# x kept by heads and turned with the unit matrix, quarters of w1 and w2 in halves, nine raw buffers for the first pieces

## The chip, the cores and the metric

One core of one Trainium2 chip. The metric is device time in microseconds (us) of one execution of the whole kernel, as the median of several runs. The engines are named as the profile names them: PE (TensorE: matmuls), PEld (its weight loads), DVE (VectorE), ACT (ScalarE), POOL (GpSimd), SP (SyncE, which here issues most DMAs).

## The reference

```python
def reference(x, state, w1, w2, w3, w_out, w_gate, w_val, w_out2):
    # x: 8 batches, 8 heads, 512 positions, 64; state: 8, 8, 32, 64
    a = softmax(scale * x @ state.T)          # 512 x 32 of each batch and head
    xread = a @ state
    a2 = softmax(scale * state @ x.T)         # 32 x 512
    sread = a2 @ x
    t = concatenate([xread, sread], axis=2)   # 8 x (512 + 32) rows = 4352 rows of 512
    h = ((t @ w1) * (t @ w2)) @ w3            # 512 -> 1024 -> 1024
    y = h @ w_out                             # 1024 -> 512
    return (sigmoid(y @ w_gate) * (y @ w_val)) @ w_out2     # 512 -> 1536 -> 512
```

x and state come in as float32, the weights of the two feed-forward blocks as float64, which the kernel turns into float32 by itself.

## The kernel before

The kernel has two large parts. The first goes through the eight batches in turn: the attention of a batch and the first feed-forward block of its 512 rows. The second does the second feed-forward block. PE works in order; what it is given, and in which order, is written out by hand.

**The batches.** While a batch's feed-forward block runs (`ffn1`, eight steps `j` with matmuls into `pab`, then four steps with matmuls into `py`), the attention of the next batch is put between its steps: `attention` returns small functions, and the dictionary `before` puts them into numbered slots. Slots 6 and 7 hold `xt`, two calls in each: one call turns two heads of x, so that the 64 columns of a head lie on partitions. Before the change one call is four transposes on PE of 128x128 (`turn`, line 289), for which x lies as `xn[p, pair, chunk, head of the pair, 64]`; ACT then copies the result to `xT`. Slot 8 holds `scores` (line 312, matmuls into `psc` on 64x32 parts of the array) and the softmax, and slots of the batch after it `a2t` (line 404), `sread` (line 421, `psr`, 128x32 parts) and `sreadt`. The products of state and weights (line 526, `psw`, 64x32 parts) are made there too: each `make(0, 1)` or `make(2, 3)` turns two quarters of w1 and w2 into the weights of the next batch, and `fetch` has the quarters loaded again from DRAM (`w12_d`).

x of a later batch is loaded by `load_x`, one DMA for each of the eight heads.

**The first batch.** `plan_start` has no other work to hide behind. It lists its steps with an engine, a cost in microseconds and what each depends on, and `Plan.order` turns the list into one order for all engines: among the steps that can begin first it takes the one with the longest path behind it. The engines then run what they got in order. In it

- `load_half` loads x in two DMAs as `xz`, and `place_x` lets ACT copy it into `xn` in four copies, one for each pair of heads; the turn of a pair waits for its copy (`placed`);
- `convert` loads one piece of 128x512 float64 numbers into a raw buffer and turns it into float32 (ACT: lines 196 and 197, DVE: lines 198, 202, 206). There are 40 such pieces: 16 of w1 and w2, 8 of w_out, 16 of w3. The raw buffers are a ring of seven (`raws`, `raw_tile`): three in the pool `cv`, two in `pw`, and two that later hold `aT`;
- `quarter(q)` converts four pieces into one tile `wq` (two such tiles), and has POOL store the tile to `w12_d` (line 656) as soon as it is full;
- `make(q)` multiplies a quarter with the state and `pab(j)` multiplies the result with the attention weights; in the first batch both are plain float32;
- `wo_split` splits a piece of w_out into a high part (ACT, tile `wo0`) and a low part (DVE, line 808, tiles `wol` on the places with the tag `sw1`), `w3_turn` turns and splits w3, and `wp_sum` multiplies the two (`pwp`); `u_split` splits the products of the first batch.

Of the kernel before, what the change touches and what calls it, by code (L numbers as in the profile page):

```python
# [8 lines left out]
F32 = mybir.dt.float32  # L9
# [108 lines left out]
def tile_state_attention__then__gated_ffns(  # L118
# [145 lines left out]
    with tc.manual_schedule(engines={mybir.EngineType.PE}):  # L264
# [3 lines left out]
        xn = {}  # L268

        def load_x(b):  # L270
            t = at.tile([P, G, SC, 2, D], F32, name="xn", bufs=2)
            xn[b] = t
            for h in range(H):
                nc.sync.dma_start(
                    out=t[:, h // 2, :, h % 2], in_=x[b, h].rearrange("(p c) d -> p c d", c=SC)
                )

        def attention(b, plain=False):

# [3 lines left out]
            def xt(g):  # L283
                def turn():
                    if g == 0:
                        t["xT"] = at.tile([P, G, S], F32, tag="xT", name="xT")
                    pt = t["pxt", g] = ps_at.tile([P, 512], F32, tag="at", name="pxt")
                    for c in range(SC):
                        nc.tensor.transpose(
                            pt[:, c * P : (c + 1) * P],  # L290
                            xn[b][:, g, c].rearrange("p a d -> p (a d)"),
                            ident,
                        )

                return [
                    ("pe", 0.44, turn),
                    ("act", 0.49, lambda: copy("act", t["xT"][:, g], t["pxt", g])),
                ]
# [116 lines left out]
            def sread():  # L415
                def products_():
                    pt = t["psr"] = ps_at.tile([P, 2, D], F32, tag="at", name="psr")
                    for k in range(2):
                        for c in range(SC):
                            for g in range(G):  # L420
                                nc.tensor.matmul(
                                    pt[NS * g : NS * g + NS, k],
                                    t["a2"][:, k, c, NS * g : NS * g + NS],
                                    xn[b][:, g, c, k],
                                    start=c == 0,
                                    stop=c == SC - 1,
                                )
# [67 lines left out]
            )  # L495

        def new_wq():
            return pb.tile([P, 2, G, WQ], F32, name="wq", bufs=2)

        def fetch(q):  # L500
            t = new_wq()
            nc.sync.dma_start(
                out=t.rearrange("p a g f -> p (a g f)"), in_=w12_d[q].rearrange("p a g f -> p (a g f)")
            )
            return t

        def behind(fn):
            with tc.issue_after(last["raw"].ins):
# [2 lines left out]
        class StateWeights:  # L511
# [9 lines left out]
            def product(self, q, pts):  # L521
                w = self.raw.pop(q)
                for a in range(2):
                    for g in range(G):
                        for k in range(2):
                            nc.tensor.matmul(
                                pts[k][NS * g : NS * g + NS, a * WQ : (a + 1) * WQ],
                                stT[64 * k : 64 * k + 64, g, self.b * NS : (self.b + 1) * NS],
                                w[64 * k : 64 * k + 64, a, g],
                                start=True,  # L530
                                stop=True,
                            )
# [27 lines left out]
        def plan_start(cur, nxt):  # L560
# [1 line left out]
            plan = Plan()  # L562
            add = plan.add
            b = cur.b
            raws, rs, ms, wqs = Ring(7), Ring(2), Ring(3), Ring(2)
            ats, mains, ys_, asbs, w3s = Ring(2), Ring(4), Ring(2), Ring(2), Ring(3)
            cell = {}

            def chain(parts, *deps):
                for engine, cost, fn in parts:  # L570
                    deps = (add(engine, cost, fn, *deps),)
                return deps[0]

            def raw_tile(n):
                if n % 7 < 3:
                    return cv.tile([P, 512, 2], U32, name="raw", bufs=3)
                if n % 7 < 5:
                    return pw.tile([P, 512, 2], U32, name="raw", bufs=2)
                return at.tile([P, 512, 2], U32, tag=f"aT{n % 7 - 5}", name="raw")

            def convert(src, place, *deps):
                n = len(raws.users)
                raw_free, raw_users = raws.take()
                r_free, r_users = rs.take()
                c = {}

                def load():
                    c["raw"] = raw_tile(n)
                    load_raw(c["raw"], src)

                def first():
# [20 lines left out]
                for j in range(4)  # L612
            ]

            def load_half(i):
                if i == 0:
                    cell["xz"] = at.tile([P, H, SC, D], F32, tag="xn", name="xz", bufs=2)
                h = i * H // 2
                nc.sync.dma_start(
                    out=cell["xz"][:, h : h + H // 2].rearrange("p h c d -> p h (c d)"),  # L620
                    in_=x[b, h : h + H // 2].rearrange("h (p c) d -> p h (c d)", c=SC),
                )

            xs = [add("sp", 0.48, lambda i=i: load_half(i), load=1.7) for i in range(2)]

            def place_x(g):
                if g == 0:
                    xn[b] = at.tile([P, G, SC, 2, D], F32, name="xn", bufs=2)
                copy("act", xn[b][:, g], cell["xz"][:, 2 * g : 2 * g + 2].rearrange("p a c d -> p c a d"))

            placed = []
            for g in range(G):
                placed.append(add("act", 0.52, lambda g=g: place_x(g), xs[g // 2], *placed[-1:]))

            wq_users = []

            def quarter(q):
                free, users = wqs.take()
                wq_users.append(users)
                out = []  # L640

                def place(i):
                    if i == 0:
                        cur.raw[q] = cell["wq", q] = new_wq()
                    a, h = divmod(i, 2)
                    return cell["wq", q][:, a, 2 * h : 2 * h + 2].rearrange("p g f -> p (g f)")

                for i in range(4):
                    a, h = divmod(i, 2)
                    src = (w1, w2)[a][2 * h * P : 2 * (h + 1) * P, 2 * q * WQ : 2 * (q + 1) * WQ]  # L650
                    d, _ = convert(src.rearrange("(k p) f -> p k f", p=P), lambda i=i: place(i), free, *out[:1])
                    out.append(d)

                def store():
                    t = cell["wq", q]
                    nc.gpsimd.dma_start(
                        out=w12_d[q].rearrange("p a g f -> p (a g f)"),
                        in_=t.rearrange("p a g f -> p (a g f)"),
                    )

                users.append(add("pool", 1.0, store, out, load=2 * LOAD))
                return out

            turned = []
            for g in range(G):
                free, users = ats.take()
                parts = xt(g)
                p = chain(parts[:1], free, placed[g])
                turned.append(chain(parts[1:], p))
                users.append(turned[-1])  # L670
            free, users = mains.take()
# [119 lines left out]
            for k in range(HALF):  # L791
                wo_load(k)
            w3_load(0)
            pab(6)
            pab(7)

            wo = {}

            def wo_tile(k, i):
                if "wo" not in cell:  # L800
                    cell["wo"] = pw.tile([P, JF, DM], F32R, name="wo0", bufs=1)
                    cell["wol"] = [
                        pb.tile([P, 2, DM], F32R, tag="sw1", name="wol", bufs=4) for _ in range(JF // 2)
                    ]
                return cell["wol"][k // 2][:, k % 2] if i else cell["wo"][:, k]

            def minus(o, x0, x1):
                nc.vector.tensor_tensor(out=o, in0=x0, in1=x1.bitcast(F32), op=ALU.subtract)

            def wo_split(k):  # L810
                a = add("act", 0.52, lambda: copy("act", wo_tile(k, 0), cell["wof", k]), wof[k])
                wo[k] = a, add(
                    "dve", 0.6, lambda: minus(wo_tile(k, 1), cell["wof", k], wo_tile(k, 0)), a
                )
# [90 lines left out]
            def u_split(j):  # L905
# [8 lines left out]
                a = add("act", 0.52, high, uw[j], [wo[k] for k in range(JF)], *cell.get("us", []))  # L914
                cell["us"] = [add("dve", 0.6, lambda: minus(t[1], cell["uw", j], t[0]), a)]

            for j in range(JF):
                u_split(j)

            add("sp", 6.7, lambda: load_x(order[1]), placed, load=3.0)  # L920
            for q in range(2):
                add("sp", 0.5, lambda q=q: nxt.fetch(q), wq_users[q + 2], load=3.0)

            engines = mybir.EngineType
            with tc.manual_schedule(
# [62 lines left out]
        class DirectWeights:  # L988
# [5 lines left out]
            def prep(self, j):  # L994
                q, jj = divmod(j, 2)
                if q not in self.raw:
                    self.raw[q] = fetch(q)
                f = self.raw[q][:, :, :, jj * P : (jj + 1) * P]
                t = [pb.tile([P, 2, KM, P], F32R, tag=f"sw{i}", name=f"dw{i}", bufs=4) for i in range(2)]
                for a in range(2):  # L1000
                    split(t[0][:, a], t[1][:, a], f[:, a])
                self.done[j] = t

            def weights(self, j):
# [633 lines left out]
```

## Time and profile before

| | us |
|---|---|
| median of 3 runs (1331.62 to 1333.92) | 1332.9 |
| the profiled execution | 1333.85 |
| its span, first to last instruction | 1332.1 |
| PE busy in it | 1299.9 (98%) |
| DVE busy | 847.7 (64%) |
| ACT busy | 678.9 (51%) |
| mean granted TensorE clock | 0.993 |

The profiled execution lies 0.95 us above the median. A busy PE is one that always has a matmul in flight. The share of the granted clock is of 2.4 GHz; 0.50 is 1.2 GHz.

### The profile page before, as it was taken

To read this page: it belongs to the slowest core of one execution; us is meant where nothing else is said; L and a number is where in the kernel's file an instruction comes from. 1 tells how busy PE (TensorE), PEld (TensorE's weight loads), DVE (VectorE), ACT (ScalarE), POOL (GpSimd) and SP (SyncE) were. 2 spreads that over 40 slices of the span, in tenths; PEclk is the share of its full clock that TensorE was granted. 3 is DMA by queue.
4 is the path that set the end of the run, shared out by engine and by line. 5 is a ranking of instruction groups with operands and counts; after the bars stand their busy time and mean duration, and the time that the engine had idled before them with its cause. 6 is when DMAs were issued, how large, how long until landed. Compare 5 with 4: busy or idle time off the path is not lost. (4 is left out here: it accounts for less than half of the span.)

```text
span 1332.1 us, 20278 instructions
## 1 busy us (share of the span) xinstructions
PE 1299.9 (98%) x7664; PEld 1090.8 (82%) x7664; DVE 847.7 (64%) x1519; ACT 678.9 (51%) x1347; POOL 133.9 (10%) x155
## 2 busy tenths in 40 slices
PE   4999999999999999999999999999999999999997
PEld 2487777778777779988899998888998988889995
DVE  5893554574574685186767776858777756657643
ACT  5993444455454574364555664643654542524521
POOL 0000000020202030012222101222211000000000
PEclk7999999999999999999999999999999999999999
DMA  8994342345463542824434567546355744133122
GB/s 292 347 279 132 114 156 73 142 150 196 170 206 143 214 171 85 316 90 149 139 127 162 176 258 266 174 141 219 135 194 190 277 181 162 48 127 126 52 95 71
DMA packets 122185, 224.67 MB, mean 169 GB/s; under 512 B 39912, under 2 KB 68072, under 8 KB 115432
## 3 DMA queue, kind: packets, MB, share of 16 engines
q1 hardware_dynamic: 87464, 163.08, 35.6%
q10 hardware_dynamic: 32896, 46.67, 10.2%
q0 software_dynamic: 1728, 13.63, 2.6%
q8 instruction: 60, 0.98, 0.3%
q14 instruction: 37, 0.30, 0.1%
HBM read 155.19 MB, written 68.16 MB: 168 GB/s over the span
## 5 line engine op out<-in xcount | busy, mean ns | idle before, releaser
L1425 PE MATMUL psA<-y,wt 128*128 128x384 f32 (+1 forms) x1440 | 301.0, 357 | 0.7 <-ACT sg L1450 0.5
L1522 PE MATMUL po<-wo,p 128*128 128x512 f32 x1224 | 281.3, 390 | 0.8 <-DVE p L1086 0.8
L1425 PEld LDWEIGHTS psA<-y,wt 128*128 128x128 f32 x1440 | 259.1, 188 | 25.3 <-ACT sg L1450 0.8
L1522 PEld LDWEIGHTS po<-wo,p 128*128 128x128 f32 x1224 | 229.2, 188 | 49.5 <-DVE p L1086 2.5
L1425 PE MATMUL psB<-y,wt 128*128 128x384 f32 (+1 forms) x720 | 159.5, 356 | 0.0
L158 ACT ACTIVATE u<-psA 128x384 f32<-128x384 f32 (+1 forms) x120 | 63.9, 532 | 159.1 <-PE psA L1425 140.3
L1425 PEld LDWEIGHTS psB<-y,wt 128*128 128x128 f32 x720 | 130.0, 188 | 11.2
L225 PE MATMUL py<-u,wp 128*128 128x512 f32 (+1 forms) x576 | 132.3, 381 | 0.8 <-DVE u L163 0.6
L225 PE MATMUL pab<-aT,sw 128*128 128x512 f32 x448 | 126.6, 404 | 0.8 <-DVE aT L163 0.8
L225 PEld LDWEIGHTS py<-u,wp 128*128 128x128 f32 x576 | 102.9, 188 | 26.2 <-issue 2.9
L964 DVE TENSOR_TENSOR asb<-asb,pab 128x512 f32<-128x512 f32 (+1 forms) x64 | 41.8, 653 | 115.7 <-PE pab L228 106.3
L158 ACT ACTIVATE p<-sg 128x384 fp32r<-128x384 f32 (+1 forms) x120 | 67.9, 567 | 80.6 <-DVE sg L1461 68.8
L163 POOL TENSOR_TENSOR o<-m,o 128x256 fp32r<-128x256 f32 x72 | 60.7, 843 | 436.1 <-ACT o L158 358.1
L225 PEld LDWEIGHTS pab<-aT,sw 128*128 128x128 f32 x448 | 81.1, 188 | 19.5 <-DVE aT L163 1.1
L1537 DVE TENSOR_TENSOR ob<-po,ob 128x512 f32<-128x512 f32 x68 | 46.7, 688 | 62.3 <-PE po L1522 59.3
L1452 DVE TENSOR_TENSOR sg<-psB,u 128x384 f32<-128x384 f32 (+1 forms) x60 | 36.4, 607 | 75.8 <-ACT u L158 75.7
L1425 PE MATMUL psC<-y,wt 128*128 128x384 f32 (+1 forms) x360 | 80.0, 357 | 0.3 <-DVE s L1458 0.2
L1086 DVE TENSOR_TENSOR p<-sg,p 128x384 fp32r<-128x384 f32 (+1 forms) x120 | 74.1, 617 | 3.9 <-ACT p L158 0.8
L1086 DVE TENSOR_TENSOR y<-yf,y 128x384 fp32r<-128x384 f32 (+1 forms) x112 | 68.3, 634 | 12.7 <-ACT y L158 11.5
L228 PE MATMUL pab<-aT,sw 128*128 128x512 f32 x224 | 70.6, 396 | 0.0
L1425 PEld LDWEIGHTS psC<-y,wt 128*128 128x128 f32 x360 | 64.8, 188 | 6.6 <-DVE s L1458 1.1
L158 ACT ACTIVATE y<-yf 128x384 fp32r<-128x384 f32 (+1 forms) x120 | 62.1, 556 | 11.3 <-DMA yf<-yd 10.5
(128 smaller groups left out, 1795.8 us busy)
## 6 DMA issues: line engine op xcount, KB each, us to landing
wq<-w12d SPq DMA_DIRECT2D x32, 1024.0 KB, 6.8
wt<-wd SPq DMA_DIRECT2D x12, 1792.0 KB, 9.0
part<-ob SPq DMA_DIRECT2D x68, 256.0 KB, 2.6
ob<-part SPq DMA_DIRECT2D x68, 256.0 KB, 3.7
raw<-in_moe_w SPq DMA_DIRECT2D x32, 512.0 KB, 5.6
wd<-o ACTq DMA_DIRECT2D x56, 256.0 KB, 2.1
yf<-yd SPq DMA_DIRECT2D x27, 384.0 KB, 3.9
yf<-yd SPq DMA_DIRECT2D x19, 512.0 KB, 4.7
```

The lines of the kernel that those rows point to most:

```text
L158: return nc.scalar.activation(out=o, in_=i, func=AF.Copy)
L163: (sub or nc.vector).tensor_tensor(out=lo, in0=src, in1=hi.bitcast(F32), op=ALU.subtract)
L225: nc.tensor.matmul(o, w[i], xx[k], start=begin and n == 0 and i + k == 0, stop=False)
L228: nc.tensor.matmul(o, w[1 - late], xx[late], start=False, stop=end and n == len(pairs) - 1)
L964: p2["dve"] = nc.vector.tensor_tensor(out=asb[:, :n], in0=asb[:, :n], in1=pab[1][:, :n], op=ALU.mult)
L1086: nc.vector.tensor_tensor(out=o, in0=x0, in1=x1, op=ALU.subtract)
L1425: nc.tensor.matmul(o, w[:, i, kb * P : (kb + 1) * P], xx[kb][h], start=start, stop=i == 1 and kb == 1, skip_group_check=True,)
L1452: nc.vector.tensor_tensor(out=t, in0=o, in1=kept[a, what], op=ALU.add)
L1522: nc.tensor.matmul(o, pt[j][i][:, s * P : (s + 1) * P], wot[j][:, h], start=j == js[0] and i + h == 0, stop=j == js[-1] and i == 1,)
L1537: nc.vector.tensor_tensor(out=ob, in0=o, in1=ob, op=ALU.add)
```

## The change

x now stays in one layout from load to use, `xn[p, head, chunk, 64]`, in every batch. It is loaded in two DMAs of four heads each, and the copies of `place_x` are gone. The turn of two heads is eight matmuls instead of four transposes: the 128x64 numbers of one head and one chunk are the weights, the 128x128 unit matrix is what moves, and the two heads of a pair go to the lower and the upper 64 partitions of the result. `sread` reads the new layout.

A quarter of w1 and w2 is now two tiles (w1's part and w2's part) of half the size, on four places. In `plan_start` quarters 0 and 1 lie there, quarters 2 and 3 on the four places tagged `sw1`. `fetch` and the stores to `w12_d` are two DMAs for each quarter where they were one. The stores of quarters 2 and 3 stand after the first piece of w3 in the list of steps; those of quarters 0 and 1 stand at its end and wait for the fourth piece of w_out.

The raw buffers: the first 16 pieces (w1 and w2) use nine, three in `cv`, two in `pw` and four on places tagged `wo0`; the 24 others use five, `cv` and `pw`. The high part of w_out, one tile before, is four tiles on the `wo0` places. `wo_split` of an even `k` therefore waits for the last user of the raw buffer there, and for the product and the stores of quarter 2 (`k` below 4) or quarter 3.

```diff
         def load_x(b):
-            t = at.tile([P, G, SC, 2, D], F32, name="xn", bufs=2)
-            xn[b] = t
-            for h in range(H):
-                nc.sync.dma_start(
-                    out=t[:, h // 2, :, h % 2], in_=x[b, h].rearrange("(p c) d -> p c d", c=SC)
-                )
+            for i in range(2):
+                load_half(b, i)
+
+        def load_half(b, i):
+            if i == 0:
+                xn[b] = at.tile([P, H, SC, D], F32, name="xn", bufs=2)
+            h = i * H // 2
+            nc.sync.dma_start(
+                out=xn[b][:, h : h + H // 2].rearrange("p h c d -> p h (c d)"),
+                in_=x[b, h : h + H // 2].rearrange("h (p c) d -> p h (c d)", c=SC),
+            )
...
                     for c in range(SC):
-                        nc.tensor.transpose(
-                            pt[:, c * P : (c + 1) * P],
-                            xn[b][:, g, c].rearrange("p a d -> p (a d)"),
-                            ident,
-                        )
+                        for k in range(2):
+                            nc.tensor.matmul(
+                                pt[D * k : D * k + D, c * P : (c + 1) * P],
+                                xn[b][:, 2 * g + k, c],
+                                ident,
+                                start=True,
+                                stop=True,
+                            )
...
         def new_wq():
-            return pb.tile([P, 2, G, WQ], F32, name="wq", bufs=2)
+            return pb.tile([P, G, WQ], F32, name="wq", bufs=4)
...
-            raws, rs, ms, wqs = Ring(7), Ring(2), Ring(3), Ring(2)
+            rs, ms = Ring(2), Ring(3)
...
+            def raw_slot(n):
+                if n < 4 * NQ:
+                    n %= 9
+                    return ("cv", n) if n < 3 else ("pw", n - 3) if n < 5 else ("wo", n - 5)
+                n = (n - 4 * NQ) % 5
+                return ("cv", n) if n < 3 else ("pw", n - 3)
...
-            placed = []
-            for g in range(G):
-                placed.append(add("act", 0.52, lambda g=g: place_x(g), xs[g // 2], *placed[-1:]))
...
-                users.append(add("pool", 1.0, store, out, load=2 * LOAD))
                 return out
+
+            def store(q, *deps):
+                for a in range(2):
+                    def go(a=a):
+                        nc.gpsimd.dma_start(
+                            out=w12_d[q][:, a].rearrange("p g f -> p (g f)"),
+                            in_=cell["wq", q][a].rearrange("p g f -> p (g f)"),
+                        )
+                    wq_users[q].append(add("pool", 1.0, go, quarters[q], *deps, load=LOAD))
...
-                p = chain(parts[:1], free, placed[g])
+                p = chain(parts[:1], free, xs[g // 2])
...
             w3_load(0)
+            store(2)
+            store(3)
             pab(6)
...
             def wo_split(k):
-                a = add("act", 0.52, lambda: copy("act", wo_tile(k, 0), cell["wof", k]), wof[k])
+                if k % 2 == 0:
+                    cell["free", k // 2] = [raw_slots.get(("wo", k // 2)), wq_users[2 + k // 4]]
+                a = add(
+                    "act", 0.52, lambda: copy("act", wo_tile(k, 0), cell["wof", k]), wof[k],
+                    cell["free", k // 2], wo[k - 1] if k % 2 else None,
+                )
...
+            store(0, wof[HALF - 1])
+            store(1, wof[HALF - 1])
             for j in range(JF):
                 u_split(j)
 
-            add("sp", 6.7, lambda: load_x(order[1]), placed, load=3.0)
+            add("sp", 1.7, lambda: load_x(order[1]), turned, load=3.0)
             for q in range(2):
-                add("sp", 0.5, lambda q=q: nxt.fetch(q), wq_users[q + 2], load=3.0)
+                add("sp", 0.5, lambda q=q: nxt.fetch(q), wq_users[q], load=3.0)
```

## Rows read from the trace of the kernel before

**Rows 1.** The page, part 1: busy us, share of the span, instructions.

```profile
PE 1299.9 (98%) x7664; PEld 1090.8 (82%) x7664; DVE 847.7 (64%) x1519; ACT 678.9 (51%) x1347; POOL 133.9 (10%) x155
```

**Rows 2.** Busy us (instructions) of each engine by stretch, granted clock, DMA share, GB/s.

```profile
70.00:80.00 10.00, 10.00 (x51) 8.24 (x50) 10.00 (x22) 9.51 (x17) 0.00 (x0) 1.00 0.87 294
...
400.00:450.00 50.00, 50.00 (x413) 39.28 (x412) 27.05 (x44) 27.72 (x50) 9.69 (x10) 1.00 0.47 169
```

**Rows 3.** PE in order of time, first and last turn slot: start us, us, instructions.

```profile
119.23 1.09 PE L289 MATMUL pxt<-ident,xn 128*128 128x128 f32 x8
120.08 3.89 PE L225 MATMUL py<-u,wp 128*128 128x512 f32 x16
...
436.31 1.03 PE L289 MATMUL pxt<-ident,xn 128*128 128x128 f32 x8
437.11 1.18 PE L225 MATMUL pab<-aT,sw 128*128 128x512 f32 x4
```

**Rows 4.** Lines 289, 421, 312, 526: duration ns min/median/max, first and last start.

```profile
L289 PE MATMUL pxt<-ident,xn x128: 270/272/476, 7.5 to 437.1; 128*128 128x128 f32 x128
L421 PE MATMUL psr<-xn,a2tr x512: 218/219/244, 46.8 to 479.9; 128*32 128x64 f32 x171
L312 PE MATMUL psc<-xT,stT x128: 588/602/616, 13.2 to 440.6; 64*32 64x512 f32 x128
L526 PE MATMUL psw<-wq,stT x1024: 375/376/632, 14.6 to 455.5; 64*32 64x256 f32 x171
```

**Rows 5.** PE in order of time, products on parts of the array.

```profile
173.63 1.09 PE L312 MATMUL psc<-xT,stT 64*32 64x512 f32 x16
174.51 1.93 PE L526 MATMUL psw<-wq,stT 64*32 64x256 f32 x64
176.38 3.92 PE L225 MATMUL py<-u,wp 128*128 128x512 f32 x16
...
212.61 1.10 PE L421 MATMUL psr<-xn,a2tr 128*32 128x64 f32 x64
213.64 1.20 PE L225 MATMUL pab<-aT,sw 128*128 128x512 f32 x4
```

**Rows 6.** All engines in order of time, the start, with idle time before them.

```profile
6.75 1.15 ACT L158 ACTIVATE xn<-xz 128x512 f32<-128x512 f32 x2 [3.76 <-DMA xz<-in_x]
7.53 1.94 PE L289 MATMUL pxt<-ident,xn 128*128 128x128 f32 x8 [7.53 <-ACT xn L158]
...
9.43 0.46 DVE L198 TENSOR_SCALAR r<-raw 128x512 uint16<-128x512 uint16 x1 [9.43 <-DMA raw<-in_moe_w]
...
12.16 0.43 DVE L202 TENSOR_SCALAR wq<-wq 128x512 uint32<-128x512 uint32 x1 [2.27 <-ACT wq L196]
...
13.15 1.09 PE L312 MATMUL psc<-xT,stT 64*32 64x512 f32 x16 [0.69 <-ACT stT L158]
...
13.81 0.69 DVE L206 CUSTOM_DVE_ANT_0 wq<-wq,r 128x1024 uint16<-128x1024 uint16 x1 [1.23 <-ACT r L197]
...
25.52 1.24 DVE L386 STREAM_TRANSPOSE a2tr<-st 128x1024 f32<-128x1024 f32 x1
...
26.90 9.86 PE L219 MATMUL pab<-a2tr,swp 128*128 128x512 f32 x16 [2.87 <-DVE a2tr L386]
```

**Rows 7.** Busy us by stretch, as in rows 2, around the clock's rise.

```profile
31.00:32.00 1.00, 1.00 (x2) 0.34 (x1) 0.01 (x1) 1.00 (x3) 0.00 (x0) 0.50 0.98 346
33.00:34.00 1.00, 1.00 (x3) 0.38 (x2) 0.97 (x3) 1.00 (x3) 0.53 (x1) 1.00 0.62 182
```

**Rows 8.** POOL's and ACT's order of time, then DMA issues with median us to landing.

```profile
43.96 1.10 POOL L656 DMA_DIRECT2D w12d<-wq  x1 [10.44 <-DVE wq L206]
...
53.65 0.68 ACT L158 ACTIVATE wo<-wof 128x512 fp32r<-128x512 f32 x1
...
w12d<-wq POOLq DMA_DIRECT2D x4, 1024.0 KB, 8.2
```

**Rows 9.** Who waited for DMAs that load raw, over the whole span: us, times.

```profile
  DMA raw<-in_moe_w: 9.4, 1
```

More of the change, by code (lines that the diff above doesn't have):

```diff
@@ L423, in products_ @@
                                     t["a2"][:, k, c, NS * g : NS * g + NS],
-                                    xn[b][:, g, c, k],
+                                    xn[b][:, 2 * g + k, c],
                                     start=c == 0,
@@ L497, in new_wq @@
         def new_wq():
-            return pb.tile([P, 2, G, WQ], F32, name="wq", bufs=2)
+            return pb.tile([P, G, WQ], F32, name="wq", bufs=4)
         def fetch(q):
[L501 to L505, printed above, removed]
+            out = []
+            for a in range(2):
+                out.append(new_wq())
+                nc.sync.dma_start(
+                    out=out[a].rearrange("p g f -> p (g f)"),
+                    in_=w12_d[q][:, a].rearrange("p g f -> p (g f)"),
+                )
+            return out
         def behind(fn):
@@ L528, in product @@
                                 stT[64 * k : 64 * k + 64, g, self.b * NS : (self.b + 1) * NS],
-                                w[64 * k : 64 * k + 64, a, g],
+                                w[a][64 * k : 64 * k + 64, g],
                                 start=True,
@@ L564, in plan_start @@
             b = cur.b
-            raws, rs, ms, wqs = Ring(7), Ring(2), Ring(3), Ring(2)
+            rs, ms = Ring(2), Ring(3)
+            raw_slots = {}
             ats, mains, ys_, asbs, w3s = Ring(2), Ring(4), Ring(2), Ring(2), Ring(3)
-            cell = {}
+            cell = {"raws": 0}
             def chain(parts, *deps):
@@ L572, in chain, with raw_tile @@
                 return deps[0]
-            def raw_tile(n):
-                if n % 7 < 3:
+            def raw_slot(n):
[4 more added lines that the diff above has]
+                return ("cv", n) if n < 3 else ("pw", n - 3)
+            def raw_tile(kind):
+                if kind == "cv":
                     return cv.tile([P, 512, 2], U32, name="raw", bufs=3)
-                if n % 7 < 5:
+                if kind == "pw":
                     return pw.tile([P, 512, 2], U32, name="raw", bufs=2)
-                return at.tile([P, 512, 2], U32, tag=f"aT{n % 7 - 5}", name="raw")
+                return pw.tile([P, 512, 2], U32, tag="wo0", name="raw", bufs=4)
             def convert(src, place, *deps):
-                n = len(raws.users)
-                raw_free, raw_users = raws.take()
+                slot = raw_slot(cell["raws"])
+                cell["raws"] += 1
+                raw_free, raw_users = raw_slots.get(slot), []
+                raw_slots[slot] = raw_users
                 r_free, r_users = rs.take()
@@ L587, in load @@
                 def load():
-                    c["raw"] = raw_tile(n)
+                    c["raw"] = raw_tile(slot[0])
                     load_raw(c["raw"], src)
@@ L613, in plan_start @@
             ]
[L615 to L629, printed above, removed]
-            placed = []
-            for g in range(G):
-                placed.append(add("act", 0.52, lambda g=g: place_x(g), xs[g // 2], *placed[-1:]))
+            xs = [add("sp", 0.48, lambda i=i: load_half(b, i), load=1.7) for i in range(2)]
             wq_users = []
             def quarter(q):
-                free, users = wqs.take()
-                wq_users.append(users)
+                wq_users.append([])
                 out = []
                 def place(i):
-                    if i == 0:
-                        cur.raw[q] = cell["wq", q] = new_wq()
                     a, h = divmod(i, 2)
-                    return cell["wq", q][:, a, 2 * h : 2 * h + 2].rearrange("p g f -> p (g f)")
+                    tiles = cur.raw.setdefault(q, [None, None])
+                    cell["wq", q] = tiles
+                    if tiles[a] is None:
+                        tiles[a] = (
+                            new_wq() if q < 2 else pb.tile([P, G, WQ], F32, tag="sw1", name="wq", bufs=4)
+                        )
+                    return tiles[a][:, 2 * h : 2 * h + 2].rearrange("p g f -> p (g f)")
                 for i in range(4):
@@ L650, in quarter @@
                     src = (w1, w2)[a][2 * h * P : 2 * (h + 1) * P, 2 * q * WQ : 2 * (q + 1) * WQ]
-                    d, _ = convert(src.rearrange("(k p) f -> p k f", p=P), lambda i=i: place(i), free, *out[:1])
+                    d, _ = convert(src.rearrange("(k p) f -> p k f", p=P), lambda i=i: place(i))
                     out.append(d)
[L654 to L659, printed above, removed]
-                users.append(add("pool", 1.0, store, out, load=2 * LOAD))
-                return out
+                return out
+            def store(q, *deps):
+                for a in range(2):
+                    def go(a=a):
+                        nc.gpsimd.dma_start(
+                            out=w12_d[q][:, a].rearrange("p g f -> p (g f)"),
+                            in_=cell["wq", q][a].rearrange("p g f -> p (g f)"),
+                        )
+                    wq_users[q].append(add("pool", 1.0, go, quarters[q], *deps, load=LOAD))
             turned = []
@@ L799, in wo_tile @@
             def wo_tile(k, i):
[L800 to L803, printed above, removed]
+                if ("wo", k // 2) not in cell:
+                    cell["wo", k // 2] = [
+                        pw.tile([P, 2, DM], F32R, tag="wo0", name="wo0", bufs=4),
+                        pb.tile([P, 2, DM], F32R, tag="sw1", name="wol", bufs=4),
                     ]
-                return cell["wol"][k // 2][:, k % 2] if i else cell["wo"][:, k]
+                return cell["wo", k // 2][i][:, k % 2]
             def minus(o, x0, x1):
@@ L810, in wo_split @@
             def wo_split(k):
-                a = add("act", 0.52, lambda: copy("act", wo_tile(k, 0), cell["wof", k]), wof[k])
+                if k % 2 == 0:
[3 more added lines that the diff above has]
+                    cell["free", k // 2], wo[k - 1] if k % 2 else None,
+                )
                 wo[k] = a, add(
@@ L997, in prep @@
                     self.raw[q] = fetch(q)
-                f = self.raw[q][:, :, :, jj * P : (jj + 1) * P]
+                f = [v[:, :, jj * P : (jj + 1) * P] for v in self.raw[q]]
                 t = [pb.tile([P, 2, KM, P], F32R, tag=f"sw{i}", name=f"dw{i}", bufs=4) for i in range(2)]
                 for a in range(2):
-                    split(t[0][:, a], t[1][:, a], f[:, a])
+                    split(t[0][:, a], t[1][:, a], f[a])
                 self.done[j] = t
```

## The prediction

> **What bounds the kernel now.** I read the page's totals first, then busy time by stretch, then PE's order of time around each place that the change touches, and last the start with its idle times. The totals [rows 1] show PE busy for 98% of the span, with DVE at 64% and ACT at 51%. By stretch [rows 2], PE is busy for all 50.00 us of 400 to 450 at a granted clock of 1.00 while DVE has 27.05 and ACT 27.72: in the batches PE alone sets the time, DVE and ACT have nearly half their time free, and a microsecond added to PE is a microsecond added to the kernel. Even at 70 to 80, in the first batch, PE has no gap, though there DVE (10.00) and ACT (9.51) are full as well. So the kernel is PE's uninterrupted work plus what passes before it begins. That beginning is at 26.90 [rows 6]: the first `pab` waits for DVE's `a2tr`, the end of the first softmax; before it PE does short pieces and waits.
>
> Two questions follow. How much PE time do the edits add to the batches? How much earlier does the first `pab` start, and does the rest of the first batch keep up?
>
> **The turn of x, seven later batches.** A slot is two calls of `xt`, before eight transposes: from 119.23 to 120.08 (0.85 us) in the first slot and from 436.31 to 437.11 (0.80) in the last [rows 3], and there are 14 (two for each of seven batches). 0.80 us for eight is 0.100 us for one that streams 128 columns.
>
> After, a slot is 2 calls x 4 chunks x 2 heads = 16 matmuls in float32, and these cost more passes than transposes. The counts show it [rows 4]: `pxt` has 128 records, which is 8 batches x 16 transposes, one each. `sread` is 32 matmuls in a batch, 256 in all, and has 512 records; `scores` is 8 in a batch, 64 in all, and has 128; the product with the state is 16 for a quarter, 512 in all, and has 1024. So a float32 matmul runs as two records and a transpose as one. A slot becomes 32 records of 128 columns. Each uses 64 columns of the array, so that two, for the two heads of a pair, can run side by side: 16 rounds where there were 8.
>
> Whether they run side by side, the products on parts of the array say [rows 5]. `psw`: 64 records of 256 columns on eight parts (64x32), which is 8 rounds, from 174.51 to 176.38, 1.87 us for 2048 columns. `psc`: 16 records of 512 columns on eight parts, 2 rounds, from 173.63 to 174.51, 0.88 us for 1024 columns. `psr`: 64 records of 64 columns on four parts (128x32), 16 rounds, from 212.61 to 213.64, 1.03 us for 1024 columns. One after the other `psc` alone would have been 16 x 512 columns at 0.100 us for 128, 6.4 us, so the parts do run together. The new slot has 16 x 128 = 2048 columns. By the transposes that is 16 x 0.100 = 1.60 us, by `psc` 1.76, by `psw` 1.87, by `psr` 2.06. I take 1.83, a little below `psw`, which has the same columns but twice the records; the ends are 1.60 and 2.06. Less the 0.80 that goes, a slot grows by 1.03 (0.80 to 1.26), and 14 slots by **14.4 us (11.2 to 17.6)**. Nothing hides it: PE is the engine that sets the end. ACT's copies to `xT` come a little later, with ACT half idle.
>
> The Trainium skill (TensorEngine Tiling (Array Packing), Key Properties) says that a change of tiling mode drains the array, and its Gotcha 2 that column tiling excludes the transpose mode for float32. The second names what the counts show, since two halves abreast could then not be transposes; the first would put the slot at the upper rows, and `psr` with its 1.03 us bears it out, as an estimate 0.1 to 0.2 us for a slot.
>
> **The start.** What goes: four copies on ACT of x; the first pair begins at 6.75 as x lands, and PE's first turn waits until 7.53 [rows 6]. What comes: PE's turns there double as well, half a slot, 0.92 us, for a pair, at clock 1.00 still. Begun at about 6.8, four pairs take PE to 10.5, the state's turn to about 10.8, ACT's copy of that to about 11.5, and `psc` begins at about 11.6, not 13.15: 1.5 us earlier. From there DVE rules: it does the softmax and the first quarter's conversions in turn and is busy almost without a break from 13.81 to `a2tr`, which begins at 25.52. Before that it had idle times of 2.27 us (to 12.16) and 1.23 us (to 13.81) [rows 6]; ACT, freed of its copies, can fill part of them with conversions. All 3.5 us filled is the most that DVE can give; the 1.5 us of `psc` less whatever the planner's new order loses is the nearer figure. I take **2 us earlier** for the first `pab`, between 3 us later and 6 us earlier. The upper end takes in the clock: `pab` begins at 1.2 GHz, still the granted clock at 31 to 32, and is at full speed from 33 [rows 7], so that up to half of some six microseconds hangs on when the clock rises.
>
> Behind that, make(1) to make(3) and `wp_sum` have to come 2 us earlier too. ACT has four copies less to do, DVE nothing less. PE runs in this part with hardly a gap, so I carry the 2 us through to the end of the first batch.
>
> **Edits that I cost at nothing.** Nine raw buffers in place of seven: over the whole trace one wait of an engine is put down to the landing of raw, the first 9.4 us [rows 9], before any buffer is used twice; a deeper ring brings nothing that anyone waited for. Five in place of seven for the last 24 pieces: hidden while a landing comes before its conversion; if that cover is gone, ACT and DVE, which are full there [rows 2], are late by what is missing, and PE after them. Later stores of quarters 0 and 1: POOL has nothing behind them but stores, and only the fetches of the second batch wait. SP's queue: two DMAs for x in place of eight, two in place of one for each quarter; PE waited for none of these in the batches.
>
> The one new wait with a price: `wo_split(0)` on ACT now waits for the stores of quarter 2. That store was issued at 43.96 and such a store lands 8.2 us later, at 52.2; the first copy to `wo` ran at 53.65 [rows 8]. So there are 1.5 us of slack, and behind the waiting copy stand ACT's next conversions and its copies for `pab`.
>
> **The sum.** Profiled execution 1333.85 + 14.4 - 2 = 1346.25. That execution lies 0.95 above the median of 1332.9, so I forecast **1345.3** for the median, about 0.9% slower.
>
> **Rivals.**
>
> *The halves don't run side by side.* Then a slot is 32 records one after the other, 32 x 0.100 = 3.2 us, 2.4 more than before, 14 slots 33.6, and the time 1332.9 + 33.6 - 2 = 1364.5. Against it: `psr` also has all 128 rows and splits the columns alone, and its 64 records took 1.03 us, where one after the other they would take 64 x 0.050 = 3.2 us. For it: no row has two parts of 64 columns. By the Trainium skill (TensorE: Matmul & The Clock Gate, Part 3, The mechanism) weight loads overlap with matmuls in flight only where the row groups differ; here both heads use all rows. That rule would bring this case, and `psr` does not bear it out. 5%.
>
> *The turn costs what it did.* If a float32 matmul against the unit matrix were one record, a slot would be 16 records side by side, 8 x 0.100 = 0.80 us, as now, and only the start would count: 1330.9, on the other side. It decides at the record count, 256 or 512 for all batches. Against it: all three other float32 products show two. 4%.
>
> *The start gives nothing, or takes.* If the new order or the wait of `wo_split` for the stores costs what `psc` gains, and ACT cannot catch up, the first batch ends 0 to 3 us later than before: 1332.9 + 14.4 + 1.5 = 1348.8. It decides when the stores of quarter 2 land later than the first copy to `wo` is due. For it: the slack of 1.5 us, and full ACT and DVE. Against it: PE needs these pieces only at `wp_sum`, some ten microseconds later. 15%.
>
> **Chances.** The forecast has 76%, and the range for it and the third rival together: from 1332.9 + 11.2 - 5 = 1339 to 1332.9 + 17.6 + 1 = 1351.5, since both ends of both terms seldom meet. Left out are the first two rivals and the tails, some 15%. A measurement of this kernel tells 0.2%, 2.7 us, from no change. Slower by more: all but the second rival and a start far better than any row allows, 94%. Within 0.2%: 3%, and faster by more, the second rival with a start at its upper end: 3%.
>
> **What would show it.** Line 289's matmuls: 512 records of 128x64 weights, and a slot from its first record to the next `pab` of 1.6 to 2.1 us. The period of a batch, slot to slot, about 2.1 us longer, with PE still without gaps. `psc` begins at 11 to 12, the first `pab` at 23 to 26. No wait of ACT for a DMA at the first copy to `wo`. The forecast is wrong if the slots stay at 0.80 us or go to 3 us, or if PE is found waiting in the batches; the start is wrong if the first `pab` is not before 26.9, or if PE shows new idle time of a microsecond or more between it and the end of the `wp_sum` stretch.

## The result and the profile after

The changed kernel takes 1350.68 us (median of 6 runs, 1347.36 to 1355.24) beside 1332.72 of the kernel before: ratio 1.0136, 95% interval 1.0122 to 1.0150, 18.0 us slower. Its runs spread wider than those of the kernel before (1331.62 to 1333.92), and the profiled one, 1355.24 with a span of 1353.5, is the longest of them.

The page's totals, as in [rows 1], then line 295 (the turn, line 289 before) by its records, as in [rows 4]:

```profile
PE 1318.3 (97%) x8048; PEld 1106.6 (82%) x8048; DVE 849.2 (63%) x1519; ACT 679.1 (50%) x1343; POOL 134.9 (10%) x159
```

```profile
L295 PE MATMUL pxt<-ident,xn x512: 272/273/474, 6.1 to 459.3; 128*64 128x128 f32 x171
```

PE has 384 records more, all of them the turn's: 512 where there were 128, as the pass count said. Two slots in the middle of a batch, PE in order of time (start us, us):

```profile
287.00 1.97 PE L295 MATMUL pxt<-ident,xn 128*64 128x128 f32 x32
288.89 1.20 PE L225 MATMUL pab<-aT,sw 128*128 128x512 f32 x4
...
291.84 1.97 PE L295 MATMUL pxt<-ident,xn 128*64 128x128 f32 x32
293.74 1.20 PE L225 MATMUL pab<-aT,sw 128*128 128x512 f32 x4
```

A slot is 1.89 to 1.90 us from its start to the next `pab`, 0.80 before [rows 3]. Yet a batch, from one `psrt` to the next, takes 55.25 us and before 53.29, which is only 1.96 more, less than two slots' 2.20. So something in the batches also got faster. From the first batch's `psrt` to the eighth's that makes 13.8 us.

The first batch ends at its `psrt`, here after the change and then before:

```profile
124.88 0.27 PE L449 MATMUL psrt<-ident,sr 128*128 128x128 f32 x1
```

```profile
116.63 0.27 PE L441 MATMUL psrt<-ident,sr 128*128 128x128 f32 x1
```

It ends 8.25 us later in the profiled run. 8.25 + 13.8 = 22.0, of the spans' 21.4 (what follows the eighth `psrt` took 0.6 less). The median lies 4.6 below the profiled run. Of the 18.0 us between the medians, 13.8 are the batches'; I put the other 4 down to the first batch of a usual run, though only the one run's trace shows that batch.

Where, in the first batch: the start, all engines, with idle time before the instruction, as in [rows 6],

```profile
6.12 6.59 PE L295 MATMUL pxt<-ident,xn 128*64 128x128 f32 x64 [6.12 <-DMA xn<-in_x]
...
13.98 1.09 PE L320 MATMUL psc<-xT,stT 64*32 64x512 f32 x16 [0.69 <-ACT stT L158]
...
14.54 0.43 DVE L202 TENSOR_SCALAR wq<-wq 128x512 uint32<-128x512 uint32 x1 [4.71 <-ACT wq L196]
...
28.04 3.75 PE L219 MATMUL pab<-a2tr,swp 128*128 128x512 f32 x4 [2.60 <-DVE a2tr L394]
```

and the waits between 27 and 90 us (who waited for whom: us in total, times, longest):

```profile
PE pwp L225 <- ACT w3t L158: 3.4, 1, 3.4
...
ACT m L196 <- DMA raw<-in_moe_w: 2.2, 2, 1.8
...
DVE r L198 <- DMA raw<-in_moe_w: 1.3, 2, 1.1
...
ACT wof L196 <- DMA raw<-in_moe_w_out: 0.7, 1, 0.7
```

The first four turns take 6.6 us, not the 3.7 of the forecast; DVE stands idle for 4.71 us where I had it filling part of its gaps; the first `pab` begins at 28.04, 1.1 us late and not 2 us early. Later ACT waits 2.9 us for raw pieces (before, nobody waited for one but the very first, [rows 9]), so `w3t` is late and PE waits 3.4 us. And behind that pause the clock is down (busy us by stretch, granted clock in the column before the last two):

```profile
70.00:71.00 1.00, 0.26 (x1) 0.26 (x2) 1.00 (x3) 1.00 (x3) 0.00 (x0) 0.54 0.79 295
71.00:72.00 1.00, 1.00 (x3) 0.81 (x4) 1.00 (x2) 1.00 (x3) 0.00 (x0) 0.50 0.61 213
72.00:76.00 4.00, 4.00 (x10) 2.96 (x10) 2.61 (x6) 0.94 (x2) 0.00 (x0) 0.50 0.60 215
76.00:77.00 1.00, 1.00 (x6) 0.97 (x5) 0.00 (x0) 0.00 (x0) 0.00 (x0) 0.54 0.07 25
```

PE is busy for some six microseconds of this at 1.2 GHz; by my estimate half of them, 3 us, are lost.

How the 8.25 us are made up, PE's busy time shows from the seventeenth record of `pab` (39.26 after, 38.65 before) to `psrt`, here after and then before:

```profile
39.26:124.88 85.62, 79.67 (x438) 55.50 (x437) 67.87 (x137) 64.15 (x115) 4.61 (x8) 0.96 0.77 264
```

```profile
38.65:116.63 77.98, 76.36 (x438) 53.54 (x437) 66.67 (x136) 64.11 (x115) 1.63 (x2) 1.00 0.83 273
```

0.6 us are lost before this stretch, 4.3 in it by longer pauses (85.62 less 79.67 is 5.95, before 1.62), and 3.3 because the same 438 records take longer, at a granted clock of 0.96 and not 1.00. So the wait for `w3t` and the clock behind it are most of the loss, and the slow turns at the start are little of it.

### The profile page after: what moved, and what is told of

Same layout as the page of the kernel before. It is cut to its first block, busy times and chain, and to the rows that moved or that the text cites. A ratio compares the mean times of both kernels' runs of the same rounds, so it can differ in the third digit from the quotient of the medians.

```text
span 1353.5 us, 21069 instructions
## 1 busy us (share of the span) xinstructions
PE 1318.3 (97%) x8048; PEld 1106.6 (82%) x8048; DVE 849.2 (63%) x1519; ACT 679.1 (50%) x1343; POOL 134.9 (10%) x159
## 3 DMA queue, kind: packets, MB, share of 16 engines
q8 instruction: 63, 1.03, 0.3%
## 5 line engine op out<-in xcount | busy, mean ns | idle before, releaser
L1442 PEld LDWEIGHTS psB<-y,wt 128*128 128x128 f32 x720 | 130.0, 188 | 11.2
L225 PE MATMUL py<-u,wp 128*128 128x512 f32 (+1 forms) x576 | 132.5, 382 | 1.2 <-DVE u L163 0.6
L225 PE MATMUL pab<-aT,sw 128*128 128x512 f32 x448 | 124.8, 400 | 0.8 <-DVE aT L163 0.8
L228 PE MATMUL pab<-aT,sw 128*128 128x512 f32 x224 | 69.2, 390 | 0.0
L228 PE MATMUL py<-u,wp 128*128 128x512 f32 (+1 forms) x288 | 67.7, 377 | 0.0
```

What stands on the lines that cost most here:

```text
L225: nc.tensor.matmul(o, w[i], xx[k], start=begin and n == 0 and i + k == 0, stop=False)
L228: nc.tensor.matmul(o, w[1 - late], xx[late], start=False, stop=end and n == len(pairs) - 1)
L1442: nc.tensor.matmul(o, w[:, i, kb * P : (kb + 1) * P], xx[kb][h], start=start, stop=i == 1 and kb == 1, skip_group_check=True,)
```

## The experiments

Each ran beside the kernel before on the same chip; ratios are to that. "First batch" is the time of its `psrt`, "batch" the distance of two later ones, both of the profiled run. The kernel before, e5 and e9 have the same steps in the first batch and differ by 1.0 us in that column (116.37 to 117.39), so that a difference of this size in it shows nothing.

| run | us | ratio (95%) | first batch | batch |
|---|---|---|---|---|
| before | 1332.7 | 1 | 116.63 | 53.29 |
| changed | 1350.7 | 1.0136 (1.0122 to 1.0150) | 124.88 | 55.25 |
| e1_old_x | 1334.8 | 1.0011 (1.0002 to 1.0020) | 120.99 | 52.83 |
| e2_turn_only | 1350.4 | 1.0134 (1.0118 to 1.0149) | 116.93 | 55.73 |
| e3_stores_early | 1347.8 | 1.0113 (1.0100 to 1.0127) | 116.66 | 55.25 |
| e4_seven_late | 1348.0 | 1.0117 (1.0103 to 1.0130) | 117.67 | 55.25 |
| e5_aT_place | 1333.1 | 1.0000 (0.9991 to 1.0009) | 116.37 | 53.31 |
| e6_full_matmul | 1347.3 | 1.0106 (1.0092 to 1.0120) | 118.38 | 55.09 |
| e7_halves_early | 1329.4 | 0.9974 (0.9964 to 0.9985) | 115.89 | 52.83 |
| e8_warm | 1329.5 | 0.9974 (0.9963 to 0.9985) | 112.53 | 53.31 |
| e9_aT_far | 1330.6 | 0.9980 (0.9970 to 0.9990) | 117.39 | 52.83 |
| e10_halves_warm | 1326.8 | 0.9954 (0.9941 to 0.9966) | 113.53 | 52.83 |

**e1_old_x and e2_turn_only: the change in two.** e1 takes the changed kernel and gives x back its eight loads, `place_x` and the transposes; e2 takes the kernel before and changes x alone. Of the edits, only one line of each is shown.

```diff
-                p = chain(parts[:1], free, xs[g // 2])   # e1; load_x, place_x and turn as before
+                p = chain(parts[:1], free, placed[g])
...
-                p = chain(parts[:1], free, placed[g])    # e2; load_x and turn as changed, no place_x
+                p = chain(parts[:1], free, xs[g // 2])
```

> The changed kernel with x as it was before: eight loads, ACT's four copies, transposes; halves, four places and nine then five raw buffers stay. Theory A (the turn costs PE 13.7 us over the later batches, and the rest of the 18 us is lost in the first batch by the other edits): about 1332.7 + 4, 1335 to 1339, the 14 slots back at 0.80 us, and PE waits again at the first wp_sum. Theory B (the whole first-batch loss comes from the slow turn at the start, which shifts the steps after it): 1331 to 1334, no wait at the first wp_sum.

> The kernel before with x alone changed: loaded by heads, no copies, turned by matmuls; quarters, stores and the seven raw buffers as before. Theory A: 1332.7 + 13.7 + about 1 for the turn at the start at 1.2 GHz, 1346 to 1348.5, slots of 1.90 us, no wait of PE at the first wp_sum beyond the 0.6 us of before. Theory B: as the changed kernel, 1349 to 1352, with a wait of some 3 us there.

The turn alone costs as much as the whole change: 1350.4. A batch of e2 is 2.44 us longer than before, the seven together 17.0, and its first batch ends only 0.3 later. That is more than the 13.7 of Theory A. The other edits alone (e1) cost 1.9 us by the medians (1.5 by the ratio), just under Theory A's range: 4.4 lost in the first batch, with a longer wait of PE at the first `wp_sum`, and 0.46 won in each of the seven batches, which neither theory had. That wait is 2.3 us in e1, 1.1 in e2 and 0.6 before; e1's row:

```profile
PE pwp L225 <- ACT w3t L158: 2.3, 1, 2.3
```

Theory B falls: e1 has no slow turn and still the wait; e2 has the slow turn and ends its first batch within 0.3 us of the kernel before.

**e3_stores_early and e4_seven_late: the late pieces.** Both are the changed kernel with one edit. There POOL issues the four stores of quarters 0 and 1 (512 KB each) in one group with the last store before them:

```profile
50.19 2.84 POOL L665 DMA_DIRECT2D w12d<-wq  x5 [2.63 <-DVE wq L206]
```

```diff
-            store(0, wof[HALF - 1])      # e3: both stand behind their quarter
-            store(1, wof[HALF - 1])
...
-                n = (n - 4 * NQ) % 5     # e4: two more, on aT's places
+                n = (n - 4 * NQ) % 7
```

> The changed kernel with the stores of quarters 0 and 1 as soon as the quarter is full. Theory S (the 2 MB of stores issued at 50 to 53 us slow the loads of the late pieces): ACT no longer waits for raw at 60 to 67 us, the first wp_sum begins within 1 us of its time in the kernel before plus the shift of the first pab, and the time falls by 3 to 5 us, to 1346 to 1348. Theory R (five raw buffers make the loads late): the waits for raw stay, 1350 to 1352.

> The changed kernel with seven raw buffers for the last 24 pieces: cv, pw and the two places of aT that the kernel before used. Theory R: loads are issued earlier, ACT no longer waits for raw at 60 to 67 us, the time falls by 3 to 5 us to 1346 to 1348. Theory S: the loads are issued earlier but land as late, waits of ACT for raw of over 1 us stay, 1349 to 1352.

Both theories hold in half: S for e3, R for e4. The first batch is back at 116.66 and 117.67, PE's wait for `w3t`, 3.4 us in the changed kernel, is 0.3 in e3 and 0.2 in e4, and the granted clock stays at 1.00 from 70 to 77 us in both:

```profile
ACT m L196 <- DMA raw<-in_moe_w: 0.5, 1, 0.5
PE pwp L225 <- ACT w3t L158: 0.3, 1, 0.3
```

```profile
PE pwp L225 <- ACT w3t L158: 0.2, 1, 0.2
```

Either remedy is enough. I read it so: five buffers leave too few loads under way when 2 MB of stores come between them; the runs show the two remedies, not the queues. Their medians are 2.8 and 2.7 us below the changed kernel's, though the intervals of the three ratios overlap; the first batch and the wait that is gone are the firmer evidence.

**e6_full_matmul: two passes or two halves?** e6 is the kernel before with this edit alone.

```diff
-                        nc.tensor.transpose(
+                        nc.tensor.matmul(
                             pt[:, c * P : (c + 1) * P],
                             xn[b][:, g, c].rearrange("p a d -> p (a d)"),
                             ident,
+                            start=True,
+                            stop=True,
                         )
```

> The kernel before with the turn by a full 128x128 matmul against the unit matrix in place of the transpose, eight for a slot, 16 records on the whole array; x's layout, loads and ACT's copies stay. Theory P (the two records of a float32 matmul are the whole price): a slot takes 1.65 to 1.75 us, the pab beside it 2.88 to 2.90, 14 slots add 12 to 13.5 us, about 1345.5. Theory T (halves of the array cost beside it, in the slot and at the change to and from it): that is the rest to the 17 us that the turn adds in the changed kernel, some 4 us. If the full matmul also takes 1.90 us and lengthens its neighbours, halves cost nothing: 1349 to 1350.

PE in order of time, first e6 and then e2 (halves), one slot and its neighbours:

```profile
279.56 0.62 PE L228 MATMUL pab<-aT,sw 128*128 128x512 f32 x2
280.02 1.95 PE L289 MATMUL pxt<-ident,xn 128*128 128x128 f32 x16
281.72 1.18 PE L225 MATMUL pab<-aT,sw 128*128 128x512 f32 x4
```

```profile
279.84 0.63 PE L228 MATMUL pab<-aT,sw 128*128 128x512 f32 x2
280.40 1.97 PE L295 MATMUL pxt<-ident,xn 128*64 128x128 f32 x32
282.30 1.21 PE L225 MATMUL pab<-aT,sw 128*128 128x512 f32 x4
```

With the whole array a slot is 1.70 us, with halves 1.90; and in e2 the last two `pab` records before the slot begin 0.56 us ahead of it, in e6 0.46. The `pab` step beside a slot is 2.98 to 3.01 us in e2, 2.88 in e6 and 2.88 to 2.89 before. Of the 2.44 us of a batch, 1.80 is the second pass and 0.64 the halves, two thirds of that in the slots and the rest at their edges. Both theories hold, P for three quarters; e6 lies 1.8 us above P's 1345.5, and its first batch, where the turn takes two passes too and the first `pab` begins 1.5 us later, ends 1.75 later. The Trainium skill (TensorEngine Tiling (Array Packing), Key Properties) has the array drain when the tiling mode changes; the longer neighbours, which halves bring and the whole array does not, agree.

**e5_aT_place and e9_aT_far: the unforeseen gain.** What e1 does to `pab` (its line 228 matmuls take 390 ns in the mean, before 396; those of `py` 389 in both) has no edit to answer for it. But since the raw buffers no longer lie on `aT`'s places, the program lays `aT` elsewhere.

```diff
+                if n == 5:                          # e5: 32 bytes further
+                    at.tile([P, 8], F32, name="pad0")
...
+                    for name, shape in (("xT", ...), ("st", ...), ("e2", ...), ...):   # e9: these first
+                        at.tile(shape, F32, name=name)
```

> The kernel before with nothing changed but the place of aT in SBUF: two tiles of 32 bytes, never used, before and behind it move it from byte 17536 of a partition to 17568, all that follows by 64. The kernels that have the raw buffers off aT's places have it at 34784 and run a batch without the turn in 52.83 us, the kernel before in 53.29, and the difference lies in the pab matmuls. Theory M (the place modulo 64 bytes, 0 before and 32 after, sets the speed of matmuls that stream aT): a batch takes about 52.8, the time falls by some 3.3 us to about 1329.5. Theory N (another place far off, other neighbours or the halves themselves): 53.29 and 1332.9 as before.

> The kernel before with nothing changed but the order in which the places of its attention tiles are laid out: xT, st, e2 and the small ones come first, so that aT lies at bytes 34784 and 38880, as in the changed kernel, not at 17536 and 21632. Theory N1 (where aT lies decides the speed of the pab matmuls): a batch takes about 52.85 us, the time falls by some 3 us to about 1329.5. Theory N2 (the halves of the quarters or what else the change does beside it): 53.3 us a batch and the time of before, 1332.7.

Line 228 by its records, first e5 and then e9:

```profile
L228 PE MATMUL pab<-aT,sw x176: 390/394/401, 201.2 to 478.6; 128*128 128x512 f32 x176
```

```profile
L228 PE MATMUL pab<-aT,sw x178: 387/389/395, 201.7 to 479.2; 128*128 128x512 f32 x178
```

32 bytes leave the batch at 53.31; the place of the changed kernel gives its 52.83 us a batch exactly and 0.20% (0.10 to 0.30%) in all. Theory M falls (e5), N1 holds (e9). What about that place matters was not found: `xT`, `st` and `e2` move in e9 too.

**e7_halves_early, e8_warm, e10_halves_warm: what can be kept.** e7 is e1 with the early stores of e3; e8 is e5 with spare matmuls at the start; e10 is e7 with such.

```diff
+            def warm_first():                       # e8, e10: before the first turn
+                cell["warm"] = ps_main.tile([P, 512], F32, tag="m", name="warm")
+                for _ in range(13):
+                    nc.tensor.matmul(cell["warm"][:, :P], ident, ident, start=True, stop=True)
...
+                        if pad and g % 2:           # in the first quarter's product
+                            pad(2 * a + g // 2) # some matmuls of 512 columns into the same tile
```

> The changed kernel with x as before (loads, copies, transposes) and the stores of quarters 0 and 1 early again; halves, four places, nine then five raw buffers stay. Theory S (late stores make the late pieces late): the first batch ends within 1 us of the kernel before, and with the pab matmuls faster by 0.46 us a batch the whole takes 1329 to 1331. Theory R (five buffers alone are enough to lose it): 1333 to 1335, with PE's wait at the first wp_sum as in the run that had only x undone.

> The kernel before with aT moved by 32 bytes and PE kept busy at the start by matmuls whose result nobody reads: 13 of the unit matrix by itself before x lands, and three of 512 columns behind three of the four parts of the first quarter's product. Theory C (turns and the first pab run at 1.2 GHz because PE idled before, 421 ns a turn where later ones take 272): the turns run at about 272 ns, the first pab at full clock from its start, 16 records in about 7.2 us in place of 9.86, and the time falls by 2 to 4 us against the run with aT moved alone, to 1326 to 1328. Otherwise the spare matmuls delay psc or psw, and the time is the same or up to 2 us longer.

> The run with halves, nine then five raw buffers, early stores and x as before (1329.4), and PE kept busy at the start: 13 matmuls of the unit matrix before x lands, then five and four of 512 columns behind the second and the fourth part of the first quarter's product. If the two gains add (the pab matmuls' 3.3 us, and the first pab at full clock, 3 us), 1326 to 1327. If the spare matmuls or the new order of the start take one of them back, 1328.5 to 1330.

e7 is 0.26% faster than before, as Theory S had it; most of it is `aT`'s place, since e9 alone has 0.20% and the intervals overlap. That the halves, the four places or the nine raw buffers give anything beside it is not shown. e8 shows the clock at the start, and Theory C holds. PE in order of time, then line 289's records in e8 and, between 7 and 9 us, before:

```profile
1.36 4.70 PE L674 MATMUL warm<-ident 128*128 128x128 f32 x26 [1.36 <-POOL ident masks.py:199]
6.69 1.18 PE L289 MATMUL pxt<-ident,xn 128*128 128x128 f32 x8 [0.63 <-ACT xn L158]
...
25.55 7.11 PE L219 MATMUL pab<-a2tr,swp 128*128 128x512 f32 x16 [0.54 <-DVE a2tr L386]
```

```profile
L289 PE MATMUL pxt<-ident,xn x16: 272/272/330, 6.7 to 9.9; 128*128 128x128 f32 x16
```

```profile
L289 PE MATMUL pxt<-ident,xn x7: 421/421/447, 7.5 to 8.8; 128*128 128x128 f32 x7
```

With PE busy before, the turns take 272 ns, not 421, and the first sixteen `pab` records 7.11 us, not 9.86 [rows 6]. The first batch ends 3.84 us earlier than in e5, the same kernel without spare matmuls, and the time is 3.65 less, within Theory C's 2 to 4 (its 1326 to 1328 had counted on a gain from the 32 bytes). e10 joins e7 and e8 and is the fastest: 1326.8, 0.46% (0.34 to 0.59%) below the kernel before, its first `pab` at 26.17 and the product behind the sixteenth at 33.20. The gains nearly add.

## Why the prediction was right or wrong

**The direction, and that the later batches make it: right.** PE has no time to spare there, and 13.8 us are lost in them, for which I had 14.4 (11.2 to 17.6). That the two lie so near is in part luck, as the next paragraph shows.

**The size of a slot: a little low, and covered by a gain that I did not foresee.** I took 1.83 us, a little below `psw`, and it is 1.90, a little above. Beside it I charged the slot alone; its edges cost about 0.1 us more each time. Together 17.0 us (e2), not 14.4. Against that stood 3.2 us (7 x 0.46) from `aT`'s new place, which came with the raw buffers that I costed at nothing. The step from "0.80 us for eight" to "16 rounds where there were 8" held: the second pass is three quarters of the cost (e6).

**The start: 2 us earlier forecast, 1.1 later in the profiled run.** The step that failed is "half a slot, 0.92 us, for a pair, at clock 1.00 still". The granted clock does read 1.00 there, but the records say otherwise. Line 295 between 8 and 9 us, and between 127 and 140:

```profile
L295 PE MATMUL pxt<-ident,xn x14: 421/421/421, 7.6 to 9.0; 128*64 128x128 f32 x14
```

```profile
L295 PE MATMUL pxt<-ident,xn x64: 272/273/323, 127.5 to 136.7; 128*64 128x128 f32 x64
```

421 ns is the 1.2 GHz level. Other 128x128 products with the unit matrix take 272 ns at 66 us in the same run, where the column reads 1.00, and mostly 421 at 76, where it reads 0.50 and, in the microsecond of its rise, 0.54:

```profile
L841 PE MATMUL pw<-ident,m x8: 272/272/273, 66.3 to 67.1; 128*128 128x128 f32 x8
```

```profile
L841 PE MATMUL pw<-ident,m x4: 401/418/421, 76.0 to 76.7; 128*128 128x128 f32 x4
```

The kernel before showed it too: its first turns are 8 records in 1.94 us [rows 6], the later ones 8 in 1.03 to 1.09 [rows 3]. I had both rows and did not compare them. With all but the last records at half speed four pairs take 6.6 us, so `psc` comes 0.8 us late in place of 1.5 early, and DVE, which I had filling part of 3.5 us of gaps, got one of 4.71.

When the records get shorter differs from run to run: from 11.9 us in this one, from 9.4 in e2 and 9.6 in e3, where the same four pairs take 5.4 to 5.5 us, `psc` begins at 12.80 and 12.91, the first `pab` at 27.13 and 27.07, and the first batch ends within 0.3 us of the kernel before. So the slow turns took away the gain that I had forecast; the loss behind it has the other cause.

**"A deeper ring brings nothing" for the first 16 pieces: no run speaks against it. "Five in place of seven for the last 24 pieces: hidden": wrong, and the larger loss.** I named the cover, "while a landing comes before its conversion", and did not price it. With 2 MB of stores moved into the same stretch it is gone: 2.9 us of ACT's waits become 3.4 of PE's and 3 of a lower clock in the profiled run. I had weighed the stores by who waits for them, not by what they meet on the way. Both signs that I had named for a wrong start came: the first `pab` is not before 26.9, and PE has new idle time of over a microsecond ahead of `wp_sum`. The third rival had this loss at 0 to 3 us and for the wrong reason: no wait of `wo_split` for its stores appears, its first copy runs at 55.24 without idle time before it. Its 1348.8 still lies nearer to the result than the forecast.

**The rivals.** The turn at its old price and the halves one after the other are both excluded: 512 records, and 1.90 us, where one after the other they would take 3.2. The rule of the Trainium skill (TensorE: Matmul & The Clock Gate, Part 3, The mechanism) that weight loads overlap only between row groups does not hold for these halves, which share all rows: 32 records with their loads took 1.90 us, and 16 on the whole array 1.70.

So 1345.3 was 5.4 us low, and that is the first batch: forecast to end 2 us earlier, it ends some 4 us later in a usual run.

## What to carry to other kernels

Where one engine sets the time of a long part, an edit that spares another engine some copies at the start and doubles this one's work on a step is paid every round: count passes by records per call in the trace before trading a transpose for a matmul. Read an engine's speed from the duration of equal records at two places, not from the clock column alone. When buffers are cut and transfers are moved in one change, look at the stretch in which they meet: here either of them without the other cost 0.2 or 0.3 us of waiting at the first `wp_sum`, and both together 3.4.

## What the runs showed of the hardware that was not expected

- The granted clock column reads 1.00 at the start while equal records take 421 ns, and 272 later; after 4.70 us of spare matmuls they take 272 at once (e8). Transposes alone bring the change too: in e7, where PE had run nothing else, they take 417 to 421 ns from 6.84 us on and 273 from 10.56.
- The matmuls of line 228 that stream `aT` take 394 ns in the median with it at byte 17536 (before) or 17568 (e5) of a partition and 389 at 34784 (e9), with nothing else changed but the layout of its pool; which neighbour or address makes it was left open.
- Two 128x64 halves side by side cost 1.90 us for 32 records where the same product on the whole array costs 1.70 for 16, and about 0.1 us more at the edges of a slot.
